# The first expert slot's tokens: chosen one batch earlier, gathered inside the attention, into a tile of their own

## The chip, the cores and the metric

The kernel runs on one core of one Trainium2 chip. The core has five engines with queues of their own: TensorE (PE in the profile), VectorE (DVE), ScalarE (ACT), GpSimd (POOL) and SyncE (SP), and 16 DMA engines. The metric is the device time of one execution in microseconds (us), the median of several runs. Where the text says "before" and "after", it means the kernel without and with the change.

## The reference

The program is an attention layer followed by a mixture of experts with two levels of choice. Cut to what matters:

```python
# q, k, v: (8 batches, 8 heads, 576, 64), s: (8, 8, 576)
cum = np.cumsum(np.maximum(s, 0.0), axis=-1)
bias = -(cum[:, :, :, None] - cum[:, :, None, :])
scores = np.where(causal, -1e9, scale * q @ k.T + np.minimum(bias, 0.0))
scores -= scores.max(-1);  attn = np.exp(scores);  attn /= attn.sum(-1) + 1e-9
x = (attn @ v)                       # rearranged to 4608 tokens x 512

g = argmax(x @ w_group)              # one of 4 groups, weight by softmax
e = argmax(x @ w_expert[g])          # one of 4 experts in it, weight by softmax
out[token] = g_w * e_w * (relu(x[token] @ w1[g, e]) @ w2[g, e])   # 512 -> 1024 -> 512
```

Each token goes to one of 16 experts. Which tokens an expert gets is known only once the attention of all 8 batches has been computed and routed.

## The kernel before, in words

**Attention** runs over 64 head steps (8 batches, 8 heads), two heads making a pair; 32 pairs in all. Per step, PE computes the scores twice: once transposed to find each row's maximum (`pm`, line 214, read on DVE by `most()`, line 222, which adds the mask, keeps the maximum and writes the masked scores to a scratch tile `mx` that nobody reads), once for the exponentials (`ps`, lines 269 and 271; ACT writes `pt` and `pu`, line 279; POOL zeroes the triangle above the diagonal, line 288). PE then multiplies by the values (`po`, line 309), ACT takes the result out of PSUM (`vals` and `sums`, lines 313 and 316), DVE divides (lines 335 to 354), and the result `xT` is both turned back into rows (`px`, line 398, copied out by ACT and stored to the DRAM array `xs`) and split in a high and a low part (`xTh`, `xTl`) for the routing.

**Routing** of a batch is a generator, `Router.batch`, of which a token in the order table advances one piece at a time. Its pieces in the order of the program: logits `lg`, `plt`, group and expert choice on DVE (lines 783 to 804), a count of the tokens of each expert on PE (`pc`, line 811), positions (lines 828 to 853), and two products that drop each token's number into a list at its expert's place: `pi` (the numbers, two pieces of them, line 866, from `val`, line 859) and `pw` (the weights, three pieces, from `val`, line 914). Between them lie the softmax weights (lines 887 to 905).

**Experts.** `moe()` works through slots, each an expert with a number of tokens. For slot 0 the expert with the most tokens so far is chosen while the attention is still running (`first()`, at 418 us of the profile), since its 2 + 2 MB of weights take long to come. Slot 0 takes 256 of its tokens from batches 0 to 6; a further 128 (`Tile "r"`) and slot 1 follow once batch 7 is routed. `start()` writes the tokens' numbers into `st.ids0` (line 621), picks slot 1's expert and corrects the count. Two indirect DMAs on POOL's queue (line 951) then gather the 256 rows from `xs` into `xg0`; PE transposes them (`px0`, line 1043), ACT and DVE split them (`xh`, `xl`, lines 1044 and 1045), PE multiplies them with the first weights (`ph`, line 1093: per column block `f` a part with the high part of the weights and a part with the low part), ACT and DVE take the result as `hh` and `hl` (lines 1088 and 1089), and the second weights follow (`py`, line 1148). ACT rounds the weights (`wh`, line 992), and POOL, or DVE, takes the rest (`wl`, lines 995 and 1001). `pur` (line 1235) is the first product of the tile "r", with the low part `xlr` (line 1225).

**What sets the order.** Up to head step 62 all five engines follow a table written by hand, a string of tokens for each step. After that only PE's order is written by hand; the instructions of the other four are put in order by a scheduler that knows what each reads and writes, and so are the expert slots after the first ones. Tiles come from pools, and a tile's next use waits for the last reader or writer of the one before it in the same place. Before the change `xg0` lies in a pool that opens only behind the attention.

## Time and profile before

| | us |
|---|---|
| three runs | 940.46, 945.64, 947.15 |
| median | 945.64 |
| the profiled execution | 939.42 |
| its span, from the first to the last instruction | 937.7 |
| PE busy, of the span | 867.3 (92%) |
| DVE, ACT, POOL busy | 702.2, 608.3, 615.0 |

The profiled execution is a fourth run and the shortest; 1.72 us of it lie outside the span. The three timed runs differ among themselves by 0.7%. All positions below ("at 452 us") are microseconds from the start of the span.

### The profile page before, as it was taken

How to read it: one execution, taken by the hardware profiler on the slowest of the kernel's cores; microseconds unless marked ns; L12 is line 12 of the kernel's file. 1: busy time of each engine (PE TensorE's matmuls, PEld its weight loads, DVE VectorE, ACT ScalarE, POOL GpSimd, SP SyncE). 2: the span in 40 equal slices, each digit the busy share in tenths (PEclk: the TensorE clock that was granted, in tenths of full speed). 3: DMA queues.
4: the chain of work that ended last, by engine and by line, in shares of the span. 5: the costliest groups of instructions: out<-in, count | busy, mean ns of one | idle time of the engine just before them, and what ended most of it. 6: DMA issues, size and time to landing. Idle time of an engine off the chain costs nothing. (4 is left out here: it accounts for less than half of the span.)

```text
span 937.7 us, 17973 instructions
## 1 busy us (share of the span) xinstructions
PE 867.3 (92%) x5648; PEld 779.6 (83%) x5648; DVE 702.2 (75%) x2002; ACT 608.3 (65%) x1382; POOL 615.0 (66%) x732
## 2 busy tenths in 40 slices
PE   4889999999999999998887999999999999999993
PEld 3677788888878787886686999999999999999992
DVE  7546685877868685876487578998888899888830
ACT  5567677776777677767734556667676666766740
POOL 9656576665757576534875447666768778878750
PEclk9989999999999999999998999999999999999997
DMA  6999989888989889723646345455554556655510
GB/s 188 237 209 228 213 218 227 198 223 188 226 204 223 215 210 231 175 68 114 207 139 210 134 162 192 165 190 208 184 194 180 204 185 226 226 201 188 195 44 23
DMA packets 80502, 174.66 MB, mean 186 GB/s; under 512 B 9580, under 2 KB 42988, under 8 KB 72208
## 3 DMA queue, kind: packets, MB, share of 16 engines
q1 hardware_dynamic: 70496, 153.52, 57.6%
q0 software_dynamic: 7488, 18.89, 5.7%
q10 hardware_dynamic: 2416, 1.03, 0.5%
q8 instruction: 47, 0.77, 0.4%
q14 instruction: 55, 0.45, 0.2%
HBM read 108.97 MB, written 19.69 MB: 137 GB/s over the span
## 5 line engine op out<-in xcount | busy, mean ns | idle before, releaser
L995 POOL TENSOR_TENSOR wl<-raw,wh 128x512 fp32r<-128x512 f32 x182 | 233.5, 1303 | 63.7 <-ACT wh L992 48.1
L222 DVE CUSTOM_DVE_ANT_0 mx<-pm,mask 128x192 bf16<-128x192 f32 (+4 forms) x320 | 129.3, 421 | 51.2 <-PE pm L214 47.5
L992 ACT CAST wh<-raw 128x512 fp32r<-128x512 f32 x256 | 153.8, 616 | 9.8 <-issue 9.2
L1093 PE MATMUL ph<-xl,wh 128*128 128x256 f32 (+13 forms) x512 | 145.0, 303 | 4.0 <-DVE xl L1065 3.6
L1093 PE MATMUL ph<-xh,wh 128*128 128x256 f32 (+13 forms) x512 | 144.1, 301 | 1.9 <-ACT xh L1064 1.1
L269 PE MATMUL ps<-WA 68*128 68x320 f32 (+4 forms) x384 | 136.0, 358 | 8.6 <-ACT pu L279 4.0
L214 PE MATMUL pm<-WA 66*128 66x288 f32 (+4 forms) x384 | 125.9, 356 | 18.4 <-DMA WA<-ch 10.4
L309 PE MATMUL po<-pt,VT 128*128 128x256 f32 (+3 forms) x512 | 122.2, 356 | 4.8 <-ACT sums L316 2.9
L1148 PE MATMUL py<-hl,wh 128*128 128x256 f32 (+13 forms) x448 | 112.7, 302 | 0.3 <-DVE hl L1089 0.3
L1148 PE MATMUL py<-hh,wh 128*128 128x256 f32 (+13 forms) x448 | 112.7, 301 | 0.0
L271 PE MATMUL ps<-WB 128*128 128x320 f32 (+4 forms) x384 | 110.2, 300 | 0.0
L1194 DVE STREAM_TRANSPOSE yr<-yT 32x384 f32<-32x384 f32 (+1 forms) x208 | 104.5, 502 | 4.3
L309 PE MATMUL po<-pu,VT 128*128 128x320 f32 (+1 forms) x384 | 106.3, 385 | 0.0
L1060 DVE STREAM_TRANSPOSE xt<-xg 32x256 f32<-32x256 f32 (+1 forms) x208 | 102.5, 493 | 3.2
L288 POOL TENSOR_SCALAR_AFFINE_SELECT pt<-pt 128x128 f32<-128x128 f32 (+2 forms) x192 | 65.0, 348 | 59.7 <-ACT pt L279 57.1
L309 PEld LDWEIGHTS po<-pt,VT 128*128 128x128 f32 x512 | 87.7, 192 | 18.4 <-issue 4.5
L1093 PEld LDWEIGHTS ph<-xl,wh 128*128 128x128 f32 x512 | 96.6, 189 | 7.3 <-DVE xl L1065 5.4
L1093 PEld LDWEIGHTS ph<-xh,wh 128*128 128x128 f32 x512 | 96.7, 189 | 3.9 <-ACT xh L1064 2.5
L1088 ACT ACTIVATE hh<-ph 128x256 fp32r<-128x256 f32 (+13 forms) x128 | 53.7, 420 | 66.4 <-PE ph L1093 65.7
L371 POOL TENSOR_TENSOR xTl<-xT,xTh 128x512 fp32r<-128x512 f32 x30 | 38.2, 1273 | 89.1 <-ACT xTh L367 81.6
L214 PEld LDWEIGHTS pm<-WA 66*128 66x128 f32 (+1 forms) x384 | 69.2, 192 | 32.0 <-DVE mc L222 15.3
L156 POOL TENSOR_TENSOR WB<-r,hl 64x576 fp32r<-64x576 f32 x62 | 87.2, 1406 | 5.3 <-DMA WB<-hl 2.4
(245 smaller groups left out, 2002.0 us busy)
## 6 DMA issues: line engine op xcount, KB each, us to landing
raw<-in_w_dram SPq DMA_DIRECT2D x64, 1024.0 KB
r<-in_qk_dram SPq DMA_DIRECT2D x32, 576.0 KB
WA<-hl SPq DMA_DIRECT2D x61, 288.0 KB
WB<-hl SPq DMA_DIRECT2D x61, 288.0 KB
VT<-in_v_dram SPq DMA_DIRECT2D x32, 384.0 KB
WB<-hl SPq DMA_DIRECT2D x64, 144.0 KB
xs<-xr SPq DMA_DIRECT2D x15, 512.0 KB
WA<-cumd SPq DMA_DIRECT2D x56, 4.5 KB
```

Of the source, the lines that this page charges most:

```text
L156: (nc.vector if p < 1 else nc.gpsimd).tensor_tensor(out=hl[:, 2] if part else WB[p % NBB][0:64, KA, h], in0=r[hr, part], in1=hl[hr, part]. ...
L214: nc.tensor.matmul(ps[:rows, :cw], WA[i][0:66, QA, h, QO + q0:QO + q0 + rows], WA[i][0:66, KA, h, QO + c0:QO + c0 + cw], start=True, stop= ...
L222: nc.vector.tensor_tensor_reduce(out=tmp[:rows, :cw], in0=ps[:rows, :cw], in1=mk[:rows], scale=1.0, scalar=-3.0e38 if c0 == 0 else mo, op0 ...
L269: nc.tensor.matmul(ps[:rows, o:o + w], WA[i][0:68, KA, h, QO + k0:QO + k0 + rows], WA[i][0:68, QA, h, QO + q0:QO + q0 + w], start=True, st ...
L271: nc.tensor.matmul(ps[:rows, o:o + w], WB[p % NBB][:, KA, h, k0:k0 + rows], WB[p % NBB][:, QA, h, q0:q0 + w], start=False, stop=True)
L309: nc.tensor.matmul(po[0][:, qa - base:qb - base], VT[p % NVT].rearrange("p t a d -> p (t a d)")[:, (3 * t + 1 + h) * 64:][:, 0:P], x[:, c: ...
L992: self.casts.append(nc.scalar.copy(h[:, j], raw[:, j]))
L995: self.low = nc.gpsimd.tensor_tensor(out=l[:, j], in0=raw[:, j], in1=h[:, j].bitcast(F32), op=ALU.subtract)
L1060: V.transpose(dst[:, 0:n, :, j], src[:, 0:n, :, i])
L1093: self.product = nc.tensor.matmul(pss[f][:, :cap], w[f // 4][:, c, (f % 4) * P:(f % 4 + 1) * P], x[:, c, :cap], start=(c == 0 and w is sel ...
L1148: self.product = nc.tensor.matmul(pss[c][:, :cap], w[2 + f // 4][:, f % 4, c * P:(c + 1) * P], x[:, f, :cap], start=(f == 0 and w is self. ...
L1194: V.transpose(dst[:, 0:n, :, i], src[:, 0:n, :, j])
```

## The change

It does four things. `xg0` becomes a tile of the constants, 6 KB of each partition, so it exists from the beginning, and POOL zeroes it at attention step 1. `start()` is no longer an item of its own in the router's queue behind batch 6; it runs inside batch 6's routing right behind the product `pi` of that batch, and issues the two gathers itself, ahead of the rest of what it does. The scratch tile `mx` of the row maximum has one buffer in place of two, and the 20-row tile `lo` shares the place of another tile, which makes the room. Batch 6's routing gets one more piece ahead of `pw`.

```diff
--- before.py
+++ after.py
@@ -74,6 +74,7 @@
     st.key = cst.tile([P, E], F32, name="key")
     st.t3 = cst.tile([P, E, E], F32, name="t3")
     st.cst = cst
+    st.xg0 = cst.tile([P, 3, DM], F32, name="xg0")
     st.routed = None
     st.listed = {}
 
@@ -218,7 +219,7 @@
                 mo = m[P - rows:, h * NB + j:h * NB + j + 1]
 
                 def most():
-                    tmp = sm.tile([P, 512], BF16, name=f"mx{n}_{j}_{c0}", tag="mx", bufs=2)
+                    tmp = sm.tile([P, 512], BF16, name=f"mx{n}_{j}_{c0}", tag="mx", bufs=1)
                     nc.vector.tensor_tensor_reduce(out=tmp[:rows, :cw], in0=ps[:rows, :cw], in1=mk[:rows],
                                                    scale=1.0, scalar=-3.0e38 if c0 == 0 else mo,
                                                    op0=ALU.add, op1=ALU.max, accum_out=mo)
@@ -385,8 +386,6 @@
         def route(b):
             if b == B - 2:
                 rt.queue.append(rt.first())
-            if b == B - 1:
-                rt.queue.append(rt.start())
             rt.queue.append(rt.batch(b, xtail.pop(b), *xhl.pop(b)))
 
         def rows_out(p):
@@ -567,6 +566,8 @@
                     pop(part)
             for f, *args in pre.get(step, ()):
                 f(*args)
+            if step == 1:
+                nc.gpsimd.memset(st.xg0, 0.0)
             if step == -1:
                 nc.sync.dma_start(cumd, cumh.bitcast(F32))
                 rt.operands()
@@ -591,6 +592,12 @@
         manual.close()
 
 
+def gather(nc, xs, xg, r, t, ids, n=NTOK):
+
+    return nc.gpsimd.indirect_dma_start(out=xg[:r, t], out_offset=None, in_=xs[0:n], bounds_check=n - 1,
+                                        in_offset=bass.IndirectOffsetOnAxis(ap=ids, axis=0), oob_is_err=False)
+
+
 def order_key(nc, st):
 
     V = nc.vector
@@ -732,6 +739,9 @@
         nc, sm, st = self.tc.nc, self.sm, self.st
         V = nc.vector
         first_ids(nc, sm, st, 0, 2, ((0, 0, 2, st.ids0[:, 0:2]),))
+        yield
+        for t in range(2):
+            st.gathered = gather(nc, self.xs, st.xg0, P, t, st.ids0[:, t:t + 1], NTOK - S)
         self.pick(1)
         t = sm.tile([P, E], F32, name="ku")
         V.tensor_scalar(out=t, in0=st.count, scalar1=-1.0, scalar2=256.0, op0=ALU.mult, op1=ALU.add)
@@ -752,7 +762,7 @@
         lT = self.lT
 
         lg = self.logits(b, xh, xl, range(3, 4) if b in self.lg else range(4))
-        lo = sm.tile([20, 512], F32, name=f"lo{b}", tag="lo", bufs=1)
+        lo = sm.tile([64, 512], F32, name=f"lo{b}", tag="xrt", bufs=1)[:20]
         nc.scalar.copy(lo, lg[32:52])
         yield
         V.tensor_tensor(out=lT[:, 0:512], in0=lg[:20], in1=lo, op=ALU.add)
@@ -876,6 +886,10 @@
         pi = listed(0, 2, "pi")
         if b == B - 1:
             st.routed = first_ids(nc, sm, st, 0, 3, ((0, 2, 3, st.ids0[:, 2:3]), (1, 0, 3, st.ids1)))
+        if b == B - 2:
+            yield
+            for _ in self.start():
+                yield
 
         nc.scalar.activation(ex, df, AF.Exp)
         yield 1
@@ -913,6 +927,8 @@
                 else:
                     V.tensor_tensor(out=val[:, 2 + j], in0=colf, in1=c3p[:, j].unsqueeze(2).to_broadcast(C4), op=ALU.mult)
         yield 2
+        if b == B - 2:
+            yield
         listed(2, 5, "pw")
 
 
@@ -947,10 +963,6 @@
         def bc(t, ax, shape):
             return t.unsqueeze(ax).to_broadcast(shape)
 
-        def gather(xg, r, t, ids, n=NTOK):
-            return nc.gpsimd.indirect_dma_start(out=xg[:r, t], out_offset=None, in_=xs[0:n], bounds_check=n - 1,
-                                         in_offset=bass.IndirectOffsetOnAxis(ap=ids, axis=0), oob_is_err=False)
-
         def scatter(y, ids, free=False):
 
             i = nc.gpsimd.indirect_dma_start(out=out, in_=y, in_offset=None, bounds_check=NTOK - 1, oob_is_err=False,
@@ -1030,7 +1042,7 @@
             def gather(self):
                 for t, r in enumerate(self.rows):
 
-                    self.last = gather(self.xg, r, t, self.ids[:r, t:t + 1], NTOK if self.u else NTOK - S)
+                    self.last = gather(nc, xs, self.xg, r, t, self.ids[:r, t:t + 1])
 
             def x_items(self):
                 u, cap = self.u, self.cap
@@ -1207,7 +1219,7 @@
                 self.u, self.w, self.xg, self.ids, self.cw = u, w, xg, ids, cw
 
             def gather(self):
-                self.last = gather(self.xg, P, 2, self.ids)
+                self.last = gather(nc, xs, self.xg, P, 2, self.ids)
 
             def items(self):
                 u, w = self.u, self.w
@@ -1261,17 +1273,16 @@
             for f in items:
                 f()
 
-        xgs = [(x2 if i else x1).tile([P, 3, DM], F32, name=f"xg{i}") for i in range(2)]
+        xgs = [st.xg0, x2.tile([P, 3, DM], F32, name="xg1")]
         yT = sp.tile([P, 4, 384], F32, name="yT", bufs=1)
-        for x in xgs:
-            nc.gpsimd.memset(x, 0.0)
+        nc.gpsimd.memset(xgs[1], 0.0)
 
 
         ids = mc.tile([P, E, NL], I32, name="ids")
         cws = mc.tile([P, E, NL], F32, name="cws")
         wts = [Expert(0, st.e0[0:1, 0:1]), Expert(1, st.e0[0:1, 1:2])]
         first = Slot(0, wts[0], 256, xgs[0], st.ids0[:, 0:2], cws[:, 0])
-        first.gather()
+        first.last = st.gathered
         rest = Tile("r", wts[0], xgs[0], st.ids0[:, 2:3], cws[:, 0, 2:3])
         run(wts[0].load((st.evac, st.xh, st.xrt, st.xrt), (first.last,) * 4, nc.gpsimd))
         rest.gather()
```

What the engines are handed changes as follows. In the names, `po62_1` is the value product of head step 62 (the last but one), part 1, and `po63_0` and `po63_1` are those of the last step; `px29` to `px31` are the rows of the last three pairs, `px0_0` to `px0_3` the transposes of slot 0's tokens, `ph0_0` its first product; `_74` and the like are the program's buffer numbers.

POOL, around head steps 62 and 63, before:

```order
L288 AFFINE_SELECT pt1_119<-pt1_119 128x128
L911 TENSOR_TENSOR val6_6258<-col6_6242,c36_6318 128x320
L371 TENSOR_TENSOR xTl28_6184<-xT29_6309,xTh28_6183 128x512
L288 AFFINE_SELECT pu1_120<-pu1_120 128x128
L1267 MEMSET xg0_6614 128x1536
L288 AFFINE_SELECT pt1_119<-pt1_119 128x2x128
L951 DMA xg0_6614<-xs_60,ids0_69 128x512 x2
L995 TENSOR_TENSOR wl0_0_6639<-raw0_0_6637,wh0_0_6638 128x512 x4
```

and after (each line number of the kernel is some 1 to 12 higher):

```order
L289 AFFINE_SELECT pt0_118<-pt0_118 64x64
L597 DMA xg0_74<-xs_60,ids0_69 128x512 x2
L925 TENSOR_TENSOR val6_6260<-col6_6244,c36_6363 128x320
L289 AFFINE_SELECT pt1_120<-pt1_120 64x64
L289 AFFINE_SELECT pt1_120<-pt1_120 128x128
L289 AFFINE_SELECT pu1_121<-pu1_121 128x128
L289 AFFINE_SELECT pt1_120<-pt1_120 128x2x128
L372 TENSOR_TENSOR xTl28_6186<-xT29_6330,xTh28_6185 128x512
L1007 TENSOR_TENSOR wl0_0_6639<-raw0_0_6637,wh0_0_6638 128x512 x4
```

The two gathers have moved ahead of the last head step's triangles and of `val6`, and the memset of `xg0` is gone from here.

PE, from the end of the attention to slot 0's first product, before:

```order
L309 MATMUL po63_1_6378<-pt1_119,VT1_116 128x320
L398 MATMUL px29_6380<-ident_61,xT29_6309 128x128 x4
L309 MATMUL po63_1_6378<-pt1_119,VT1_116 128x192
L309 MATMUL po63_1_6378<-pt1_119,VT1_116 128x64
L309 MATMUL po63_1_6378<-pu1_120,VT1_116 128x320 x2
L398 MATMUL px30_6405<-ident_61,xT30_6389 128x128 x4
L1043 MATMUL px0_0_6730<-ident_61,xg0_6614 128x128 x2
L1043 MATMUL px0_1_6735<-ident_61,xg0_6614 128x128 x2
L398 MATMUL px31_6417<-ident_61,xT31_6412 128x128 x4
L704 MATMUL lg7_6424<-xTh28_6183,wr_sb_134 52x512
```

and after:

```order
L310 MATMUL po63_0_6396<-pu1_121,VT1_117 128x128
L1055 MATMUL px0_2_6740<-ident_61,xg0_74 128x128 x2
L1055 MATMUL px0_3_6745<-ident_61,xg0_74 128x128 x2
L310 MATMUL po63_1_6409<-pt1_120,VT1_117 128x320
L397 MATMUL px29_6411<-ident_61,xT29_6330 128x128 x4
L310 MATMUL po63_1_6409<-pt1_120,VT1_117 128x192
L310 MATMUL po63_1_6409<-pt1_120,VT1_117 128x64
L310 MATMUL po63_1_6409<-pu1_121,VT1_117 128x320 x2
L397 MATMUL px30_6436<-ident_61,xT30_6420 128x128 x4
L1105 MATMUL ph0_0_6752<-xh0_6688,wh0_0_6638 128x256
L1105 MATMUL ph0_0_6752<-xl0_6689,wh0_0_6638 128x256
```

The transposes of slot 0's tokens now stand inside the last head step: `px0_2` and `px0_3` here, and `px0_0` and `px0_1` just ahead of the first product of `po63_0`. Behind the attention's last piece slot 0's products with the high part of the weights come next, 31 of them, ahead of `px31` and the last logits `lg7`.

DVE, between the routing of batch 7 and slot 0's first layer, before (`hl0` with `ph0_4` to `ph0_7` are the last four column blocks of that layer):

```order
L848 TENSOR_TENSOR col7_6517<-hot_64,pc7_6494 128x320
L853 TENSOR_TENSOR rows7_6519<-cols_199,pc7_6494 128x640
L859 TENSOR_TENSOR val7_6521<-col7_6517,part_212 128x320 x2
L1089 SCALAR_TENSOR_TENSOR hl0_6751<-ph0_4_6812,hh0_6750 128x256
L1089 SCALAR_TENSOR_TENSOR hl0_6751<-ph0_5_6821,hh0_6750 128x256
L1089 SCALAR_TENSOR_TENSOR hl0_6751<-ph0_6_6830,hh0_6750 128x256
L872 TENSOR_TENSOR lists_63<-lists_63,pi7_6524 128x128
L1089 SCALAR_TENSOR_TENSOR hl0_6751<-ph0_7_6839,hh0_6750 128x256
```

and after:

```order
L1101 SCALAR_TENSOR_TENSOR hl0_6751<-ph0_4_6812,hh0_6750 128x256
L858 TENSOR_TENSOR col7_6525<-hot_64,pc7_6502 128x320
L863 TENSOR_TENSOR rows7_6527<-cols_200,pc7_6502 128x640
L1101 SCALAR_TENSOR_TENSOR hl0_6751<-ph0_5_6821,hh0_6750 128x256
L1101 SCALAR_TENSOR_TENSOR hl0_6751<-ph0_6_6830,hh0_6750 128x256
L869 TENSOR_TENSOR val7_6529<-col7_6525,part_213 128x320 x2
L1101 SCALAR_TENSOR_TENSOR hl0_6751<-ph0_7_6839,hh0_6750 128x256
L882 TENSOR_TENSOR lists_63<-lists_63,pi7_6532 128x128
```

The last block's `hl` (with `ph0_7`) still stands behind the two `val`, but now ahead of `lists`. On PE, 15 of the second layer's products now stand ahead of the five of `pi7` (none before), and the sixteenth, which reads that last `hl`, behind them. Further on, behind `pw7`, four DVE instructions (`sel`, `t`, `esl`, `esi`, lines 1297 to 1303 of before) now stand between `pw7` and `xlr`; before, they stood ahead of `pw7`.

## Rows read from the trace of the kernel before

**Rows 1.** Busy time by stretch: start and end of the stretch and its length in us, busy time (and number of instructions) of PE, PE's weight loads, DVE, ACT, POOL, then the granted clock of PE as a share of the full one, the busy share of the DMA engines, and GB/s.

```profile
452.00:456.00 4.00, 1.19 (x7) 0.77 (x8) 3.43 (x4) 2.33 (x5) 3.49 (x3) 1.00 1.02 328
456.00:460.00 4.00, 4.00 (x16) 1.64 (x14) 1.76 (x3) 4.00 (x10) 4.00 (x4) 0.57 0.27 68
...
600.00:800.00 200.00, 197.29 (x1398) 194.84 (x1396) 178.39 (x342) 132.29 (x274) 149.56 (x123) 1.00 0.55 193
```

**Rows 2.** PE's waits from 438 to 502 us: what waited, for which engine's or DMA's work, us in total, times, the longest.

```profile
PE pw L866 <- DVE val L914: 2.6, 1, 2.6
PE pur L1235 <- DVE xlr L1225: 2.6, 1, 2.6
PE px L398 <- DVE xT L354: 1.9, 1, 1.9
PE px L1043 <- DMA xg<-xs,ids: 1.6, 2, 1.2
```

**Rows 3.** POOL's instructions in order of time (start, duration, operation, in brackets the idle time before it and what ended it), and the last line: how long the gathers of `xg` took from issue to landing (shortest, median, longest of the six).

```profile
443.72 1.38 POOL L1267 MEMSET xg<- 128x1536 f32 x1
...
447.13 1.26 POOL L951 DMA_INDIRECT xg<-xs,ids  x1 [0.62 <-POOL pt L288]
448.70 1.00 POOL L951 DMA_INDIRECT xg<-xs,ids  x1 [0.31 <-issue]
...
479.76 1.16 POOL L951 DMA_INDIRECT xg<-xs,ids  x1 [0.30 <-issue]
...
DMA to landing us min/median/max: 3.5/3.8/5.4
```

**Rows 4.** DVE's instructions in order of time, same columns.

```profile
439.02 0.17 DVE L621 CAST ids<-kidf 128x2 int32<-128x2 f32 x1
...
471.68 2.44 DVE L859 TENSOR_TENSOR val<-col,part 128x320 bf16<-128x320 bf16 x2
474.04 1.07 DVE L1089 SCALAR_TENSOR_TENSOR hl<-ph,hh 128x256 fp32r<-128x256 f32 x3
...
479.63 0.41 DVE L1297 TENSOR_TENSOR sel<-rank,ie 128x256 bf16<-128x256 f32 x1
...
480.08 0.42 DVE L1300 TENSOR_TENSOR t<-sel,ie 128x256 f32<-128x256 bf16 x1
...
480.54 0.42 DVE L1301 TENSOR_REDUCE esl<-t 128x16 f32<-128x256 f32 x1
...
480.99 0.17 DVE L1303 CAST esi<-esl 128x16 int32<-128x16 f32 x1
481.27 1.28 DVE L914 TENSOR_TENSOR val<-col,pi 128x320 bf16<-128x320 bf16 x3
...
489.85 0.68 DVE L1225 TENSOR_TENSOR xlr<-prr_x,xhr 128x512 fp32r<-128x512 f32 x1
```

**Rows 5.** PE's instructions in order of time, same columns.

```profile
455.69 0.66 PE L398 MATMUL px<-ident,xT 128*128 128x128 f32 x4 [1.89 <-DVE xT L354]
...
461.39 0.48 PE L775 MATMUL plt<-ident,lT 20*128 20x20 f32 x5
...
472.49 2.08 PE L1093 MATMUL ph<-xh,wl 128*128 128x256 f32 x16
474.41 0.56 PE L866 MATMUL pi<-val,rows 128*128 128x128 bf16 x5
...
484.60 0.69 PE L866 MATMUL pw<-val,rows 128*128 128x192 bf16 x5
...
490.59 0.75 PE L1235 MATMUL pur<-wh,xlr 128*128 128x512 f32 x1 [2.57 <-DVE xlr L1225]
```

**Rows 6.** ACT's instructions at the end of the attention, same columns.

```profile
451.36 0.43 ACT L316 ACTIVATE sums<-po 64x320 f32<-64x320 f32 x1
451.81 2.18 ACT L992 CAST wh<-raw 128x512 fp32r<-128x512 f32 x4
```

**Rows 7.** SP's DMA issues around the choice of the first expert, same columns: the tail rows of batch 6 to `xs`, and the first weights.

```profile
425.68 0.51 SPq L770 DMA_DIRECT2D xs<-xrt  x1
...
428.11 1.01 SPq L990 DMA_DIRECT2D raw<-in_w_dram  x2
```

**Rows 8.** DVE, two row maxima back to back, and three routing instructions in a row, same columns.

```profile
305.51 0.47 DVE L222 CUSTOM_DVE_ANT_0 mx<-pm,mask 128x320 bf16<-128x320 f32 x1
...
305.92 0.34 DVE L222 CUSTOM_DVE_ANT_0 mx<-pm,mask 128x192 bf16<-128x192 f32 x1
...
462.51 0.26 DVE L788 TENSOR_TENSOR df<-plt,lmx 128x100 f32<-128x100 f32 x1
462.69 0.25 DVE L792 TENSOR_TENSOR eq<-plt,desc 128x100 f32<-128x100 f32 x1
462.97 0.27 DVE L794 TENSOR_REDUCE plt<-eq 128x25 f32<-128x100 f32 x1
```

**Rows 9.** Waits between 100 and 400 us, columns as in rows 2: the row maximum's wait for PE, and PE's wait for the row maximum.

```profile
DVE mx L222 <- PE pm L214: 32.5, 46, 1.8
...
PE pm L214 <- DVE mc L222: 3.9, 12, 0.4
```

**Rows 10.** The start of the attention: a wait of PE and a wait of ACT behind head step 1, columns as in rows 3.

```profile
47.18 0.64 PE L269 MATMUL ps<-WA 68*128 68x320 f32 x1 [1.92 <-ACT pu L279]
...
61.55 0.38 ACT L316 ACTIVATE sums<-po 64x256 f32<-64x256 f32 x1 [4.42 <-DMA WA<-th]
```


## The prediction

> **What bounds the kernel now.** Read the busy time by stretch first. In the long middle of the experts PE works 197.29 of 200 us [rows 1]: PE is the bound there, nothing in the change touches that part, and whatever the seam between attention and experts gains or loses is passed on to the end. The change therefore has to be priced in two places: at the seam, and wherever the smaller `mx` and the moved memset reach into the attention. At the seam read PE's list of waits [rows 2]. Four matter: 1.6 us until the gathered tokens land (452 to 453 us), 1.9 us until `px31` gets its `xT` (455), and, later, 2.6 us for `xlr` (488 to 490); the other 2.6 us, for `val` ahead of `pw6` (441 to 444), belongs to batch 6's routing. Then look at the clock: PE is busy 1.19 us of 452 to 456, and in the next 4 us it is busy throughout at a granted clock of 0.57 [rows 1], between the two levels of 1.2 and 2.4 GHz, so 4 x (1 - 0.57) = 1.7 us of work are lost there. All of this together, 8.7 us of waits and 1.7 of clock, is 10.4 us: even a perfect seam would give little more than 1% of the time, and 1% is about what a measurement of this kernel can tell from no change.
>
> **The gather, part by part.** The numbers it needs are ready early in the kernel before already: the cast to `ids` ends at 439.02 + 0.17 = 439.2 us, but the first gather is issued at 447.13 [rows 3, 4], behind a triangle and a memset of 1.38 us that had to wait for the pool of `xg0`. After, the gathers stand right behind `ids`. Two of 1.0 to 1.26 us each bring the second issue to an end at 441.2 to 441.7; landing took 3.5 to 5.4 us from issue [rows 3], so the rows are there by 443.8 to 445.9, where PE wants them between the last two head steps at about 443.3 (my estimate from the order and the products there). A wait of 0.5 to 2.6 us arises there; it falls into a stretch in which PE lost 2.6 us for `val` anyhow [rows 2], and `pw6`, which waits for that `val`, now stands behind `px0`, so I count it as covered, with 0 to 2.6 us for the range. POOL's other work behind the gathers, the triangles of head step 63, is delayed by the 2.3 us that the issues take and regains the memset's 1.4.
>
> A rule speaks against issuing the gathers there. The Trainium skill, in "SBUF — State Buffer", section "SBUF: two separate sides", warns that an indirect DMA issued from GpSimd has its descriptors written by GpSimd's own cores, which are locked out while DVE runs certain fast modes; under a busy DVE the issue would then stretch. The trace has the case: the gather at 479.76, between DVE instructions back to back, took 1.16 us, the one at 448.70 under an idle DVE 1.00 [rows 3, 4]. The rule would cost some 0.2 us a gather here by that row; nothing in the sum changes.
>
> **What PE does with the tokens.** The wait of 1.6 us goes. The attention's last PSUM tile leaves through ACT at 451.36 + 0.43 = 451.8, and the four `wh` casts that the first product needs take 2.18 us, 0.55 each [rows 6]; those evacuations queue behind the `xh` splits of the tokens, which I put at 0 to 0.5 us. So slot 0's products start about 452.9, and 31 of them, 16 per 1.92 us (472.49 to 474.41) or 0.12 us each, last 3.7 us [rows 5]. They fill the wait for `px31` (1.9 us, ending at 455.69), and PE is no longer idle ahead of 456, so I take the clock as full where it was 0.57. Gained: 1.6 + 1.9 + 1.7 = 5.2 us, less 0.7 for the start at 452.9 in place of the earlier end of the attention. The first layer ends **4.5 us** earlier, at 469.9 in place of 474.4.
>
> **What is late next.** That lead does not reach the end of the seam, because DVE's routing of batch 7 does not get earlier: `px31` and the logits now stand behind the 31 products, so `plt` is done at about 463.3, not at 461.39 + 0.48 = 461.9 [rows 5]. The counting product stands ahead of most low-part products now and ends at 466.3 to 467 by the 0.12 us spacing; before, DVE took it up at 467.6. The run of DVE from there to the end of `val` (471.68 + 2.44 = 474.1) took 6.5 us, of which three `hl` of 0.36 each [rows 4]. So `val` ends near 473.3, and the last `hl` behind it at 473.7. On PE the sixteenth product of the second layer reads it: fifteen go early, then PE waits from about 471.7 to 473.7. `pi` follows at 473.9 in place of 474.41: of the 4.5 us, **0.5** are left. The fifteen early products need not be done again: 15 x 0.12 = 1.8, so `pw` comes 0.5 + 1.8 = 2.3 us earlier, at 482.3 in place of 484.60 [rows 5]; its `val` is ready by then, since DVE has 1.4 us less in front of it.
>
> Then the other half of the move is paid. `sel`, `t`, `esl` and `esi`, 0.41 + 0.42 + 0.42 + 0.17 = **1.4 us**, stand behind `pw` now and ahead of `xlr` [rows 4]. From the end of `pw` (485.29) to the end of `xlr` (490.53) it took 5.2 us [rows 4, 5]; it will take 6.7. 482.3 + 0.7 + 6.7 = 489.7 for `pur`, against 490.59. **The seam gains 2.3 - 1.4 = 0.9, rounded to 1.0 us**, with -4.4 (all of the lead) and +3.3 (the second rival) as its ends.
>
> **The scratch tile.** With one buffer each row maximum waits for the write of the one before, on its own engine. What a wait on its own engine costs is seen in the routing: the instruction at 462.69 starts 0.08 us before its forerunner ends (462.51 + 0.26), the one at 462.97 waits for its forerunner's result and starts 0.03 after its end (462.69 + 0.25): 0.11 us. Two row maxima back to back overlap today in the same way, 305.92 against 305.51 + 0.47 [rows 8]. In the attention I count 96 such pairs in the trace; elsewhere other DVE work lies between. So the upper bound is 96 x 0.11 = 10.6 us, and below zero nothing speaks for a gain. But DVE waited 32.5 us for PE's scores in 300 us, PE only 3.9 us for DVE [rows 9]: the price falls into DVE's idle time nearly everywhere, and I start from the 12 places where PE did wait: over the 410 us with row maxima some 16, at 0.11 each 1.8 us. Most of these lie beside a batch's routing, where other DVE work stands between two row maxima and the wait is over before it counts; I take a quarter, **+0.4 us**.
>
> For this price, too, there is a rule. The Trainium skill, "VectorE: DVE Perf Modes", section "The DRAIN you can't avoid", reports eight copies taking the same 13.88 us with a semaphore behind each or behind the last alone. By it the wait would cost nothing and this term were 0.0; rows 8 show 0.11.
>
> **The memset.** 1.38 us of POOL [rows 3] now lie at the start, ahead of triangles that PE needs. PE waits 1.92 us for ACT there and ACT 4.42 us for a DMA a little later [rows 10], so the delay is covered but for the shape of that pile-up: 0 to 1.4, taken as **+0.2 us**. `lo` in another tile's place costs nothing that I can find: that tile is used at the other end of the routing.
>
> **Sum.** -1.0 + 0.4 + 0.2 = -0.4 us: the profiled execution would take 939.42 - 0.4 = 939.0. It is the fastest of four; their mean is (939.42 + 940.46 + 945.64 + 947.15) / 4 = 943.2, 2.4 below the median of the three. I put the change on that mean, since a new median may fall anywhere in the same spread: 943.2 - 0.4 = 942.8, said as **943 us**.
>
> **Rivals.**
> - *The lead survives.* If DVE reaches `val` earlier, or PE need not wait at the sixteenth product, `pw` comes at most 4.0 us earlier (480.6, when its own `val` is done), and 4.0 - 1.4 = 2.6 remain: -2.6 + 0.6 = -2.0, 941 us; with the 1.4 hidden as well, 4.4 and 939.4. For it: the hl of `ph0_7` misses by only 2 us. Against: 2.44 us of `val` stand ahead of it in DVE's row.
> - *The tokens come late or the clock falls.* A landing of 5.4 us [rows 3] makes PE wait 2.6 us ahead of the last head step's products, and everything behind comes later by as much: -1.0 + 2.6 = +1.6. If PE's pause ahead of 452.9 still brings the clock down as before 456 [rows 1], another 1.7 us go: +3.3. With the 0.6 of the other terms, 945.4 to 947.1.
> - *Slower: the scratch tile is not hidden.* DVE is the engine that PE runs just behind in the attention. It decides from the point at which the idle time that DVE has ahead of row maxima (32.5 us in 46 waits [rows 9], none ahead of the second of a pair) no longer reaches PE's next use: each of the 96 pairs then passes its 0.11 us on: +10.6 in place of +0.4, 943.2 - 1.0 + 10.6 + 0.2 = 953 us.
> - *It does not do what it says.* The gather reads rows of batch 6's tail from `xs`. That store was issued at 425.68, ahead of the 2 MB of weights at 428.11 [rows 7]; after, the weights go first. If the store lands late, the gather's data wait, and PE, with `px0` ahead of `po63_0`, stands still inside the attention for up to 8 us: 951.
>
> **How the numbers follow.** The forecast 0.55, the lead survives 0.22, late or slow clock 0.12, scratch tile 0.05, gather held back 0.03, something else 0.03. The range goes from 935, below the second form of the first rival (939.4) by the same 4 us that single runs lie below the mean, to 950, the highest run of before (947.15) with 2.7 of those 3.3 us on it; it leaves the last three out. Faster by over 1% would need 9.4 us, nearly all of the 10.4 there are: 0.03. Slower by over 1% is the scratch tile or the held gather, where they come out whole: 0.05. Within 1%: 0.92.
>
> **What would show it.** In the trace after: the gathers' landing no longer in PE's waits at 452 us, 31 products ahead of `px31`, the clock at 1.0 through 456 to 460; a new wait of about 2 us of PE on `hl` ahead of `pi`; `pur` waiting some 3 to 4 us for `xlr`, at 489 to 490 by the clock of before; row maxima back to back starting 0.03 us behind each other's end in place of 0.06 before it, with PE's 3.9 us of waits for them under 6. I am wrong if the attention has become longer by more than 3 us between its start and 430 us, or if the seam from the last `po` to `pur` has shrunk by over 3 us.

## The result, and the profile after

The change makes the kernel slower: 953.4 us against 945.8, medians of 18 runs each; the ratio is 1.0083, with a 95% interval of 1.0058 to 1.0109, or 7.8 us of 945 (5.5 to 10.3). The prediction of 943 had the wrong sign, and 953 lies outside its range. It is the time that its third rival gave, the scratch tile that is not hidden; that the number fits so well is luck, since the rival counted 9.8 us from a base of 943.2, nearly all of it for the tile, and measured are 7.8 from 945.8. The profiled execution of after took 955.9 us, span 954.2: 16.5 us more than that of before, twice the difference of the medians, so not each microsecond of this one trace is the change's.

First the attention. Both traces hold the same `th` (one for each head pair, on DVE), so their starts show how long a batch of four pairs takes. Start and duration of one `th` and of the fourth after it, before:

```profile
280.40 0.28 DVE L242 TENSOR_SCALAR th<-pmt 10x128 fp32r<-10x128 f32 x1 [0.42 <-PE pmt L236]
...
332.72 0.28 DVE L242 TENSOR_SCALAR th<-pmt 10x128 fp32r<-10x128 f32 x1 [0.42 <-PE pmt L236]
```

and the same two after:

```profile
291.07 0.28 DVE L243 TENSOR_SCALAR th<-pmt 10x128 fp32r<-10x128 f32 x1 [0.42 <-PE pmt L237]
...
344.18 0.28 DVE L243 TENSOR_SCALAR th<-pmt 10x128 fp32r<-10x128 f32 x1 [0.42 <-PE pmt L237]
```

A batch takes 53.1 us in place of 52.3. In a batch's steady state the change touches the scratch tile `mx`, the place of `lo` and, as a run below shows, SP's order of a few loads. What the first does is seen in two row maxima back to back, as in [rows 8]. DVE before, the instruction between the two of [rows 8]:

```profile
305.92 0.07 DVE L222 DVE_READ_ACCUMULATOR2_ANT mc<- 128x1 f32 x1
```

and all three after:

```profile
316.73 0.47 DVE L223 CUSTOM_DVE_ANT_0 mx<-pm,mask 128x320 bf16<-128x320 f32 x1
317.13 0.07 DVE L223 DVE_READ_ACCUMULATOR2_ANT mc<- 128x1 f32 x1
317.35 0.36 DVE L223 CUSTOM_DVE_ANT_0 mx<-pm,mask 128x192 bf16<-128x192 f32 x1
```

The second begins 0.62 us after the first, before it was 0.41: not 0.11 us more, as the prediction took from the routing's instructions, but 0.21. It now begins 0.15 us behind the end of the short instruction between them, which reads the maximum out; before it began together with that one. It is so throughout: in before's trace 101 row maxima (by width, 288 columns behind 448, 192 behind 448, 320 behind 288 and 192 behind 320) follow another directly and without waiting for PE, and each starts 0.05 to 0.08 us ahead of the other's end; after, 97 of the same kinds start 0.14 to 0.16 behind it.

The waits between 100 and 400 us, columns as in [rows 9]: one line of before that [rows 9] lacks, then those of after.

```profile
PEld pm L214 <- DVE mc L222: 8.8, 21, 0.5
```

```profile
DVE mx L223 <- PE pm L215: 30.0, 27, 1.8
PEld pm L215 <- DVE mc L223: 11.2, 37, 0.5
PE pm L215 <- DVE mc L223: 5.5, 18, 0.4
```

PE's own wait for the maximum rose from 3.9 to 5.5 us, that of its weight loads from 8.8 to 11.2, each time by more and not by longer waits: 18 for 12, and 37 for 21. Together that is 4.0 us more; how much of a weight load's wait reaches PE the list does not say. The time for the same work says more. From the ninth `th` to the last PE does 1845 instructions in both traces (start, end and length, PE, PE's weight loads, DVE, ACT, POOL, granted clock, DMA share, GB/s), before:

```profile
123.37:423.57 300.20, 290.70 (x1845) 243.43 (x1843) 229.17 (x887) 221.94 (x554) 187.30 (x289) 1.00 0.81 200
```

and after:

```profile
128.30:436.41 308.11, 296.98 (x1845) 246.59 (x1843) 232.51 (x887) 221.88 (x554) 187.06 (x289) 0.99 0.79 197
```

7.9 us more for 23 pairs: the prediction's own sign of being wrong, an attention longer by more than 3 us, is there. Not all of them are the tile's own: two batches of after (55.1 and 54.6 us) hold a stretch in which PE's clock was granted at half, the lower of its two levels. The traces of the experiments below bear it out: from the ninth `th` to the last the kernels with one buffer take 305.7 to 308.7 us, those with two 300.2 to 302.0; where no such stretch lies between, it is 305.7 and 305.9 against 300.2 to 300.6, some 5.5 us for 23 of the 32 pairs.

Now the seam between attention and experts. PE's waits from 440 to 508 us after, columns as in [rows 2]:

```profile
PE pur L1247 <- DVE xlr L1237: 7.7, 1, 7.7
PE pi L876 <- DVE val L869: 2.5, 1, 2.5
PE po L310 <- issue: 1.2, 1, 1.2
PE ph L1105 <- ACT wh L1004: 1.2, 1, 1.2
PE px L1055 <- DMA xg<-xs,ids: 0.8, 1, 0.8
```

Against [rows 2] the wait for the gathered tokens fell from 1.6 to 0.8, and those of `px31` for `xT` and of `pw6` are all but gone. In their place stand 1.2 us for `po63` (the list names nothing that ended it; it starts 0.1 us behind the end of an evacuation of the attention on ACT, which stood behind an `xh` cast) and 1.2 for the `wh` casts, 2.5 for `val` ahead of `pi`, where the prediction had some 2 for the `hl` behind it, and 7.7 for `xlr` where 3 to 4 were expected. On DVE and POOL, columns as in [rows 4]:

```profile
496.12 0.35 DVE L882 TENSOR_TENSOR lists<-lists,pw 128x192 f32<-128x192 f32 x1 [1.95 <-PE pw L876]
496.39 2.68 DVE L1308 TENSOR_TENSOR sel<-rank,ie 128x256 bf16<-128x256 f32 x1
...
499.45 1.29 DVE L614 SCALAR_TENSOR_TENSOR idl<-idl,xts 128x64 f32<-128x64 f32 x1
500.66 0.41 DVE L1312 TENSOR_REDUCE esl<-t 128x16 f32<-128x256 f32 x1
...
502.88 1.23 DVE L1314 CAST esi<-esl 128x16 int32<-128x16 f32 x1
...
505.75 0.68 DVE L1237 TENSOR_TENSOR xlr<-prr_x,xhr 128x512 fp32r<-128x512 f32 x1
```

```profile
495.00 3.78 POOL L1007 TENSOR_TENSOR wl<-raw,wh 128x512 fp32r<-128x512 f32 x3
499.30 4.78 POOL L1007 TENSOR_TENSOR wl<-raw,wh 128x512 fp32r<-128x512 f32 x3 [0.52 <-ACT wh L1004]
```

`sel` took 0.41 us in [rows 4] and takes 2.68 here, `esi` 1.23 in place of 0.17. `sel` ends at 499.07, just behind POOL's first three `wl` (498.78), `esi` at 504.11, just behind the next three (504.08). `esl` beside them takes its 0.41 as ever.

### The profile page after: what moved, and what is told of

It reads as the page before. It is cut to its first block, busy times and chain, and to the rows that moved or that the text cites. A ratio compares the mean times of both kernels' runs of the same rounds, so it can differ in the third digit from the quotient of the medians.

```text
span 954.2 us, 18226 instructions
## 1 busy us (share of the span) xinstructions
PE 873.1 (92%) x5648; PEld 783.0 (82%) x5648; DVE 713.6 (75%) x2002; ACT 608.0 (64%) x1382; POOL 614.8 (64%) x732
## 5 line engine op out<-in xcount | busy, mean ns | idle before, releaser
L223 DVE CUSTOM_DVE_ANT_0 mx<-pm,mask 128x192 bf16<-128x192 f32 (+4 forms) x320 | 135.1, 422 | 59.3 <-PE pm L215 41.1
L1004 ACT CAST wh<-raw 128x512 fp32r<-128x512 f32 x256 | 153.7, 615 | 10.5 <-issue 10.4
L215 PE MATMUL pm<-WA 66*128 66x288 f32 (+4 forms) x384 | 129.0, 363 | 19.4 <-DMA WA<-ch 10.0
```

The source lines that it names most:

```text
L215: nc.tensor.matmul(ps[:rows, :cw], WA[i][0:66, QA, h, QO + q0:QO + q0 + rows], WA[i][0:66, KA, h, QO + c0:QO + c0 + cw], start=True, stop= ...
L223: nc.vector.tensor_tensor_reduce(out=tmp[:rows, :cw], in0=ps[:rows, :cw], in1=mk[:rows], scale=1.0, scalar=-3.0e38 if c0 == 0 else mo, op0 ...
L1004: self.casts.append(nc.scalar.copy(h[:, j], raw[:, j]))
```

## The experiments

Ratios are to the kernel before, on the same chip, with 95% intervals.

**One buffer for `mx`, alone.**

```diff
 # the kernel before
-tmp = sm.tile([P, 512], BF16, ..., tag="mx", bufs=2)
+tmp = sm.tile([P, 512], BF16, ..., tag="mx", bufs=1)
```

> The kernel before with one change: the scratch tile mx has one buffer. Theory A (the scratch tile carries most of the loss): in the trace after, a batch's four head pairs take 0.8 us more than before (12.75 for 12.41, 12.40 for 12.18, 14.03 for 13.84, 13.9 unchanged), so over the attention about 5 us; this kernel shows the same periods and is 4 to 6 us slower than before. Theory B (the price of the prediction holds, 0.4 us, and the pair periods come from the moved tile or memset): within 1 us of before, periods as before.

Measured: 954.2 us against 945.2, ratio 1.0074 (1.0042 to 1.0106), or 7.0 us. This one number of the change gives nearly all of its loss, within the intervals all of it. The `th` four pairs apart:

```profile
238.41 0.28 DVE L242 TENSOR_SCALAR th<-pmt 10x128 fp32r<-10x128 f32 x1 [0.42 <-PE pmt L236]
...
291.74 0.28 DVE L242 TENSOR_SCALAR th<-pmt 10x128 fp32r<-10x128 f32 x1 [0.42 <-PE pmt L236]
```

53.3 us a batch, 1.0 more than before; seven to eight such batches are the 7 us.

**The change with two buffers for `mx`.**

```diff
-tmp = sm.tile([P, 512], BF16, ..., tag="mx", bufs=1)
+tmp = sm.tile([P, 448], BF16, ..., tag="mx", bufs=2)
```

> The changed kernel with two scratch tiles again, each 448 columns wide in place of 512 (no maximum is wider), which makes them fit. Theory A: the pair periods of before come back (12.4, 12.2, 13.9, 13.8), the kernel is 4 to 6 us faster than after and still 2 to 4 us slower than before, from the seam (PE's first product with xlr comes 3.1 us later there, relative to the attention) and the start. Theory B: as after, 7 to 8 us slower than before.

Measured: 946.2 us, ratio 1.0010 (0.9982 to 1.0038); 6.9 us of the 7.8 came back. A batch takes 52.3 us again:

```profile
282.40 0.28 DVE L243 TENSOR_SCALAR th<-pmt 10x128 fp32r<-10x128 f32 x1 [0.42 <-PE pmt L237]
...
334.73 0.28 DVE L243 TENSOR_SCALAR th<-pmt 10x128 fp32r<-10x128 f32 x1 [0.42 <-PE pmt L237]
```

`lo` is still in its new place here, so it is not what came back. With the buffers SP's order of a few loads moves too, here as in the run before (with one buffer a load of `WB` ahead of one of `VT` in some of the pairs). No run separates the two; against the loads as the cause speaks that PE's waits between 100 and 400 us name no DMA in before, in after or in these two runs. What is left of the change costs 0.9 us, within the interval of nothing, and less than the 2 to 4 expected.

**The memset later.**

```diff
-            if step == 1:
+            if step == 40:
                 nc.gpsimd.memset(st.xg0, 0.0)
```

> The changed kernel with the memset of xg0 at head step 40 in place of step 1. In the profile after, the fifth pair starts 5.2 us late and 3.9 of these arise between the fourth and the fifth pair. Theory C (the memset on POOL sets off the delay at the start): the fifth pair is back to within 2 us of before, and the kernel 3 to 4 us faster than after. Theory D (the start varies by itself or with mx): no change from after beyond 1 us.

Measured: 953.6 us, ratio 1.0086 (1.0055 to 1.0118), as after. Theory D: that the memset stands at step 1 costs nothing that can be seen. In this trace the fifth pair does start 3.8 us earlier than in after, yet the time did not move; in the next experiment, with the memset at step 1, the ninth pair starts at 124.2 us, here at 124.8, before at 123.4. The start differs between executions by as much.

**`sel` and what follows behind `xlr`.** The lines from `sel` to the list of all slots' tokens come in the program behind the first items of the tile "r", and are issued behind `xlr`:

```diff
+        # slot 0's products and the tile's first items are issued here
+        order = after(tc, rest.split[1])
         sel = mq.tile(S3, BF16, name="sel")
         V.tensor_tensor(out=sel, in0=bc(rank, 1, S3), in1=bc(ie, 2, S3), op=ALU.is_equal)
```

> The changed kernel with sel, t, esl, esi and the list of all slots' tokens on DVE only behind xlr. In the trace after, 7.7 us of PE's wait stand ahead of pur, and from the end of pw to xlr it takes 10.4 us against 5.2 before: 1.4 by the four instructions' own length, the rest by sel at 2.68 us in place of 0.41, idl 1.29 for 0.23, xts 1.97 for 1.23, esi 1.23 for 0.17, each of which ends when one of POOL's wl ends. Theory E (these instructions are held by POOL's wl and the whole seam loss is theirs): xlr within 2.5 us of pw, the wait ahead of pur under 1 us, the kernel 5 to 7 us faster than after, so 1 to 3 us slower than before. Theory F (the time is passed on, because the experts' weights or the next slot's tokens, which need esi and ids, come later): pur early, but a new wait of 3 us or more behind it, and less than 2 us gained.

Measured: 946.9 us, ratio 1.0007 (0.9983 to 1.0031), 7 us faster than after, with the slow `mx` still in. The wait ahead of `pur` is gone from PE's list. That is more than the whole loss of the seam in the trace: there PE's first product with `xlr` comes 70.1 us behind the last `th`, and 67.0 before, so 3.1 us later. In after 7.7 us ahead of `pur` and, further on, 5.1 ahead of `pz` (for a `wl` on DVE) make 12.8; here 2.2 ahead of `ph` (for `xl`) and 4.0 ahead of `pz` (for `done`) are left, 6.2 together:

```profile
PE pz L1190 <- DVE done L1400: 4.0, 1, 4.0
PE ph L1105 <- DVE xl L1057: 2.2, 1, 2.2
```

But the 5.1 us are no loss of the change. The kernel before has them too:

```profile
PE pz L1178 <- DVE wl L1001: 5.1, 1, 5.1
```

So Theory E has the size, but not all of it is the change's loss made good; what the same order is worth without the change, a run below tells. Of Theory F the new waits are there, but smaller than what they replace.

**POOL's `wl` held until `xlr` is done**, with `sel` where the change put it:

```diff
 self.low = nc.gpsimd.tensor_tensor(out=l[:, j], in0=raw[:, j], ...)
+if self.u == 1 and i < 2:
+    tc.add_manual_dep(self.low.ins, xlr, Sync)
```

> The changed kernel with POOL's wl of the first two weight pieces of slot 1 held until xlr is done; nothing else. It measures whether sel, idl, xts and esi are long because POOL's wl run at the same time. Theory E: sel 0.41 us, idl 0.23, xts 1.22, esi 0.17, as before where POOL was quiet, and from the end of pw to the end of xlr 6 us in place of 10.4. Rival J (they are long for a reason of their own, their operands or a wait that the trace does not show): sel above 1 us and esi 1.2 again, with no POOL instruction beside them.

One run, 947.4 us, just under the eighteen of after (947.6 to 961.9); one run gives no verdict on the time. DVE behind `pw`, and POOL's `wl`:

```profile
497.21 0.42 DVE L1311 TENSOR_TENSOR sel<-rank,ie 128x256 bf16<-128x256 f32 x1
...
498.00 0.22 DVE L614 SCALAR_TENSOR_TENSOR idl<-idl,xts 128x64 f32<-128x64 f32 x1
498.46 1.21 DVE L1329 TENSOR_TENSOR xts<-sel,idl 128x1024 f32<-128x1024 bf16 x1
499.60 0.17 DVE L1317 CAST esi<-esl 128x16 int32<-128x16 f32 x1
...
501.40 0.68 DVE L1240 TENSOR_TENSOR xlr<-prr_x,xhr 128x512 fp32r<-128x512 f32 x1
```

```profile
502.16 7.59 POOL L1007 TENSOR_TENSOR wl<-raw,wh 128x512 fp32r<-128x512 f32 x6 [7.80 <-DVE xlr L1240]
```

All four take what they took in a quiet place, and `xlr` ends 5.2 us behind the end of `pw` in place of 10.4. The own length of the four that were moved (`sel`, `t`, `esl`, `esi`) is 1.4 us, as predicted; the rest was POOL. The stretch is as short as before, though they stand in it now, in good part because before an instruction in it was held beside POOL's `wl` already, 0.97 us for what takes 0.18 here:

```profile
485.60 0.97 DVE L606 TENSOR_SCALAR xts<-idl 128x64 f32<-128x64 f32 x1
```

```profile
482.73 3.77 POOL L995 TENSOR_TENSOR wl<-raw,wh 128x512 fp32r<-128x512 f32 x3
```

The Trainium skill, "SBUF — State Buffer", section "SBUF: two separate sides", states that the port pair which GpSimd and VectorE share is an exclusive lock: whichever starts first has it for its whole instruction, against DVE's fast modes or, if GpSimd's instruction reads SBUF, DVE's with two inputs from there. The trace agrees: `sel`, `idl` and `xts` have two such inputs and were held, `esi` is a copy and was held; `esl`, a reduction, was not (0.41 in after, in the middle of POOL's run), nor was an `hl` of after with one input from PSUM, 0.41 us at 486.88 with `wl` on POOL until 488.1. It goes further in one point: `sel`, which in after begins at 496.39, in the second of three `wl` of 1.26 us each, ends only behind the third.

**Both repairs**, and **the last one on the kernel before**, without anything of the change:

> The changed kernel with both repairs: two scratch tiles of 448 columns, and sel with what follows behind xlr on DVE. Each alone took back 7 us of the 8 (946.2 and 946.9 against 945.2 for before). Theory A+E (two separate costs, the one in the attention, the other at the seam): the gains add up, 938 to 941 us, 4 to 7 us under before. Rival G (the repairs overlap, because the seam only takes what the attention leaves): 944 to 947, as each alone.

> The kernel before, nothing of the change, with sel and what follows behind xlr on DVE. It shows how much of the last run is owed to the change at all. Theory H (the early gather is worth its lead, once xlr no longer stands in the way): this kernel gains only the wait ahead of pur, 1 to 2.6 us, 943 to 944, and the last run is 3 to 5 us faster than it. Rival I (the gather's lead is lost at val, and the gain is that of the order of xlr): both within 1.5 us of each other.

Measured: both repairs 938.8 us, ratio 0.9928 (0.9899 to 0.9956), 6.8 us faster than before; `sel` behind `xlr` on the kernel before 939.7, ratio 0.9945 (0.9911 to 0.9979). The repairs add up (A+E). But the two kernels do not differ: Rival I. The early gather, with its room paid for and DVE's order mended, is worth nothing that can be measured: the means of the two differ by 0.7 us, with an interval of -2.2 to 3.5 (my estimate from the twelve times of each). PE's waits from the last `th` to `pur`, of the kernel before with `sel` late:

```profile
PE pw L866 <- DVE val L914: 2.6, 1, 2.6
PE px L1043 <- DMA xg<-xs,ids: 2.0, 2, 1.7
PE px L398 <- DVE xT L354: 1.7, 2, 1.4
PE pc L811 <- DVE hot L804: 0.5, 1, 0.5
```

and of the change with both repairs:

```profile
PE pi L876 <- DVE val L869: 2.5, 1, 2.5
PE po L310 <- issue: 1.2, 1, 1.2
PE ph L1105 <- ACT wh L1004: 1.2, 1, 1.2
PE px L1055 <- DMA xg<-xs,ids: 0.8, 1, 0.8
```

6.8 us on the one side, 5.7 on the other. The tokens' waits went, and nearly as much came in other places. `pur` even comes 65.9 us behind the last `th` with the early gather, against 64.9 without. The clock accounts for it: with the early gather it was granted at 0.85 and 0.72 from 448 to 456 us and once more at 0.69 and 0.88 from 480 to 488, together 3.4 us of work lost; without, once, at 0.59 from 460 to 464, 1.7 us.

`sel` behind `xlr` gains the kernel before 5.2 us by the ratio (2.0 to 8.4), where 1 to 2.6 were expected, the wait ahead of `pur`. The traces show what comes with it. Behind that wait the clock was low before, columns as in [rows 1]:

```profile
488.00:492.00 4.00, 1.43 (x5) 1.13 (x5) 3.97 (x6) 2.01 (x5) 3.49 (x3) 0.83 0.19 39
492.00:496.00 4.00, 4.00 (x15) 3.20 (x14) 1.60 (x5) 0.60 (x1) 1.32 (x2) 0.74 0.96 370
```

and with `sel` late, where PE no longer stands still there, it is full:

```profile
492.00:496.00 4.00, 4.00 (x22) 3.33 (x21) 4.00 (x7) 3.39 (x8) 3.45 (x3) 1.00 0.79 264
496.00:500.00 4.00, 3.73 (x23) 3.07 (x21) 3.97 (x7) 1.13 (x3) 0.54 (x1) 1.00 0.31 113
```

In each of the five traces in which `sel` stands ahead of `xlr` beside POOL's `wl` (before, after and the first three runs) the clock falls to half 66.7 to 70.7 us behind the last `th`, at the wait ahead of `pur`; with `sel` late, here, with both repairs and in the changed kernel, it does not fall there. As far as these traces show, then, the wait of PE on DVE cost more than its length, and this part of the gain has nothing to do with the change.

**`val` without POOL beside it**: as both repairs, and the four `wl` of slot 0's last weight piece wait for batch 7's `val`.

> As e5_both, with POOL's wl of slot 0's last weight piece held until batch 7's val is done. In the traces after, e3 and e4 this val (two instructions) took 3.1, 4.4 and 4.5 us while POOL's wl ran, the three of the other val 1.28 together; PE waited 2.5 to 3.9 us for it ahead of pi. Theory E, also here: val takes 0.9 to 1.2 us, PE's wait ahead of pi under 1 us, and the kernel is 2 to 3 us faster than e5. Rival K (the wl held back are missed by PE soon after): a new wait on wl among the products of the second layer, and no gain.

Measured: 939.8 us, ratio 0.9943 (0.9912 to 0.9974), no better than without. DVE and POOL:

```profile
474.06 0.88 DVE L869 TENSOR_TENSOR val<-col,part 128x320 bf16<-128x320 bf16 x2
...
488.40 5.65 DVE L1325 TENSOR_TENSOR sel<-rank,ie 128x256 bf16<-128x256 f32 x1
```

```profile
486.26 7.50 POOL L1007 TENSOR_TENSOR wl<-raw,wh 128x512 fp32r<-128x512 f32 x6
```

`val` takes 0.88 us in place of the 3.08 of after, and `pi` comes 2.0 us earlier than with both repairs, counted from the last `th`. But `pw` comes only 1.5 earlier and `pur` not at all (65.9 us behind that `th` in both); and the 1.5 is about what the clock makes, since the second stretch of half clock, 1.7 us of work lost, lies ahead of `pw` with both repairs and behind it here. The `wl` that waited ran from 475 to 480, beside the small instructions ahead of the next `val` (`kemp` and `kids`, some 0.2 us each in after, took 1.2); 1.9 us of PE's wait appear for that one, and `sel`, now behind `xlr` where it harms nobody, stood for 5.65 us until POOL's six `wl` were through. Rival K in part: nobody missed the held `wl` themselves, DVE missed the ports.

**Batch 7's logits ahead of the products**, with both repairs, and the same with the last experiment:

```diff
-            run(h[:12])
+            run(h[:3])
+            behind(tc, first.opened, st.lg)     # the third block's products behind the logits
+            run(h[3:5])
+            behind(tc, first.opened, st.plt)    # the low-part products behind plt
+            run(h[5:12])
```

> As e5_both, with PE's order at the seam changed: sixteen of slot 0's products, then px31, the logits of batch 7 and pl, sixteen more, then plt, and only then the low-part products. In e5 the 31 products, and fourteen low-part ones behind the logits, stand ahead of plt, and plt comes 40.7 us after the last th of the attention, against 37.8 in e6 without the early gather, although PE had slot 0's tokens 5 us earlier. Theory L (the seam hangs on batch 7's routing, and the early gather only gave PE work to put in front of it): plt at 37.5 to 38.5 us, pi 2 us earlier than in e5, the kernel 1 to 2 us faster than e5. Rival M (routing is not what the seam waits for): plt earlier, but pur and the slots behind it where they were, within 1 us of e5.

> As e8_both_val with the same order of PE. In e8 val took 0.88 us and pi came 2 us earlier than in e5, but pw only 1.5 and pur not at all, and the time was the same. Theory L: with plt 2 us earlier as well pur follows by 2 to 3 us, 935 to 938. Rival N (POOL's wl, moved behind val, hold the later instructions of DVE instead, so that what is gained at val is lost again at pw): pi 3 us earlier than in e5 and pur within 1 us of it, no gain.

Measured: 940.9 us, ratio 0.9920 (0.9888 to 0.9951), and 940.7, ratio 0.9926 (0.9894 to 0.9957). In the first, `plt` comes 37.8 us behind the last `th`, as without the early gather, where both repairs alone had 40.7, and `pi` 3.6 earlier; `pw` is 1.0 earlier and `pur` 1.0 earlier: Rival M. From `pi` to `pw` PE then has no wait in its list and takes 12.5 us in place of 9.9, so it has caught up with its own work. With `val` freed as well the time is the same (Rival N, though `pi` comes only 2.1 us earlier, not 3, and `pw` and `pur` 0.6 later than with both repairs). Four orders of the seam, all with `mx` in two buffers and `sel` late, lie between 0.9920 and 0.9943, within each other's intervals.

## Why the prediction was wrong

**The scratch tile (+0.4 us, measured +7.0).** The step that failed, twice. The price of one wait was taken from plain instructions of the routing, 0.11 us; between two row maxima stands the instruction that reads the maximum out, and with it the delay is 0.21. And the delay was said to fall into DVE's idle time, because DVE waited for PE 32.5 us and PE for DVE only 3.9 [rows 9]. That is a sum over 300 us and says nothing of the order of events: an idle time ahead of the first maximum of a group does not cover a delay between the first and the second, if PE's next score matmuls wait for the end of the second. That they do at 18 and 37 places is in the list of waits after; how much passes at each place was not measured. The bound of 10.6 us was right in size (96 x 0.21 would be 20; 7.0 passed); the value taken inside it was at the wrong end. The rival with 953 us named the mechanism and the point at which it decides, and got a chance of 0.05.

**The rule of the Trainium skill for that price** ("VectorE: DVE Perf Modes", section "The DRAIN you can't avoid": a semaphore between copies costs nothing) would have made it 0.0. It speaks of copies; for the row maxima the runs show 0.21 us a wait and 7.0 in all, and here the measurement decides.

**The seam (-1.0 us; +3.1 in the profile, +0.9 with an interval of -1.7 to +3.6 by the time of the change with two buffers).** In the trace of after the steps up to `pw` came as worked out: 31 products fill the wait, the clock stays at 1.0 there, `plt` slips by 1.3 us (1.4 worked out), PE waits 2.5 us ahead of `pi` (about 2), `pi` gains 0.2 (0.5) and `pw` 2.1 (2.3). Wrong was the term behind `pw`: 1.4 us for `sel` to `esi` was their length in a quiet place, but they had been moved into the time of POOL's `wl`: from the end of `pw` to the end of `xlr` it took 10.4 us, where 6.7 was worked out. [Rows 4] held the sign: `val`, two instructions in 2.44 us, where the next three take 1.28.

One trace is not the kernel, though. In us behind the last `th`, with the products that read `xlr` as `pur`, and the seam of before in the first two rows, that of the change in the other three:

| | `pi` | `pw` | end of `pw` to end of `xlr` | `pur` |
|---|---|---|---|---|
| before | 50.8 | 61.0 | 5.2 | 67.0 |
| one buffer for `mx` alone | 53.5 | 63.6 | 5.5 | 69.9 |
| after | 50.6 | 59.0 | 10.4 | 70.1 |
| the change with two buffers | 52.3 | 62.1 | 7.0 | 69.9 |
| the memset later | 52.0 | 61.8 | 7.3 | 69.8 |

In the last two the term behind `pw` is off by 0.3 and 0.6 us only (`sel` took 1.18 and 1.45 us, `esi` 1.24 and 1.23; the two instructions with two buffers are below), and it is the lead ahead of `pw` that is gone: with two buffers the clock was granted at 0.81 and 0.76 from 446 to 454 us and at 0.65 and 0.92 from 478 to 486, 3.4 us of work lost where the sum has none; with the memset later `val` took 4.42 us beside POOL's `wl`, and 1.7 us of clock went behind it. So the 1.7 us of clock in the forecast's sum are not sure to be won, and what the moved instructions cost varies with where POOL stands. The 3.1 us rest on one trace of before; the second row, the same order of the seam, has a `pur` as late as the change, with two stretches of half clock ahead of it where before had one. Whether the seam lost anything by the change stays open within the interval above; it did not gain much.

```profile
488.76 1.18 DVE L1308 TENSOR_TENSOR sel<-rank,ie 128x256 bf16<-128x256 f32 x1
...
491.92 1.24 DVE L1314 CAST esi<-esl 128x16 int32<-128x16 f32 x1
```

**The issue of the gathers** went as the prediction had it: 1.26 and 1.00 us after, under a busy DVE, and the same under an idle one before [rows 3]. What the prediction left out is that POOL's instructions hold DVE's, as `sel` and `val` show.

**The memset (+0.2)**: nothing to be seen, as far as the runs can tell.

**What the lead of the gather was worth** came out near what was argued, a lead that does not reach the end of the seam, though not for one reason. The products that it let PE do early stood in front of the logits; `val` waited for POOL's `wl`; the clock took some; and where the first two were cleared PE was at its own work.

## What to carry to other kernels

A scratch tile that nobody reads still needs its second buffer: with one, each use waits for the last, and here that made the distance of two row maxima half as long again (0.62 us for 0.41). Whether such a delay is hidden is read from what stands next to it in each group, not from sums of waits. And before an instruction of DVE is moved, see what POOL does at the new place: price it by a row where POOL is busy, not by the shortest row. And before a term is called right or wrong from one trace, look at a second one of the same order.

## What the runs showed of the hardware

An instruction of DVE with two inputs from SBUF can stand until a whole run of POOL's instructions is through, not only the one at work: `sel`, 0.42 us by itself, begun in the second of six `wl` of 1.25 us each, took 5.65 us and ended 0.3 behind the sixth. In the kernel with both repairs, where `t`, `xts` (the scaling of line 613, one input) and `idl` met three `wl`, they took 1.4, 1.3 and 1.0 us, so there each waited for about one. When which of the two happens stays open. Two row maxima with the accumulator's read between them overlap by 0.06 us if they write to different tiles, and lie 0.15 us apart, 0.21 in all, if they write to the same.
